# Routing jobs of a mixture-of-experts step moved into the half-swap of the attention matmuls

## The chip, the cores and the metric

The kernel runs on one core of a Trainium2 chip. The metric is the device time of one execution in microseconds (us). The engines are called as in the profile: PE (matmuls), PEld (its weight loads), DVE (vector), ACT (scalar), POOL (GpSimd) and SP (which only issues DMAs here).

## The reference, cut to what matters

Squared-ReLU attention without softmax, gated by u, is followed by a dense two-layer network and a top-1 mixture of eight experts on the same rows.

```python
# u, v: (8, 2816, 256)   z: (8, 2816, 64)
scores = (1.0 / S) * np.matmul(z, z.transpose(0, 2, 1))
attn = np.maximum(scores, 0.0) ** 2
x = (u * np.matmul(attn, v)).reshape(N, 256)         # N = 22528
y_dense = np.maximum(x @ w1_dense, 0.0) @ w2_dense    # 256 -> 512 -> 256
logits = x @ w_gate                                   # 8 experts
expert_idx = np.argmax(logits, axis=1)
gate_w = softmax(logits)[np.arange(N), expert_idx]
for e in range(8):
    mask = expert_idx == e
    y_moe[mask] = gate_w[mask, None] * (np.maximum(x[mask] @ w1[e], 0.0) @ w2[e])
out = y_dense + y_moe
```

## The kernel before, in words

The program is written out by a planner in Python, which keeps its own clock `now[0]` in microseconds and puts the instructions of PE, DVE, ACT and SP in a fixed order. On the chip each engine works through its list in that order.

**Attention.** The tokens stand in 176 blocks of 128, 22 to a batch element ("batch" below). Blocks of a batch are handled in groups of 2, 4, 4, 4, 4 and 4. A score call (`scores`, L368) makes up to 128x1024 scores with two or four matmuls on 64 rows each, into a pair of PSUM banks; there are four such pairs. `relu` (L390) then plans two steps for them, on ACT or DVE: scale and ReLU into a buffer (L398 on ACT, L400 on DVE), which frees the pair, and the square into the group's tile A (L411 on ACT, L413 on DVE). Part of A is had by transposing an earlier group's A with a DMA (L446). A score call may run up to two groups ahead of the group that is being used (`ahead`, L468).

`av` (L521) makes the output of two blocks, in a bank pair of its own. The upper and the lower 64 rows of the array work at the same time, each on its own bank, through 22 key blocks (44 matmuls, L548); in the second half (p = 1) the two swap banks. After every second key block stands a fill step (`fill`, L456). It takes up a waiting job if its time has come and a bank pair is free, or else a score call, if a pair is free and not too much is planned for DVE and ACT. `keep[0]` holds two pairs back towards the end of the first half.

Between the halves stands `swap_rows` (L499), which lies between the last matmul into a bank from one set of rows and the first from the other. It issues a touch (`touch`, L492: a matmul of 8 columns, tile d) and two score calls, the second in the touched pair. Where no score call is left to make (`ahead` is None), two touches in the same pair stand there.

DVE then multiplies the output by u (`gate_x`, L573, L577) into the ring `pays` of 22 blocks, and SP issues a DMA transpose of it to xT (L579).

**Routing.** The blocks are routed in 18 lots: 14 of 11 blocks, then 8, 6, 4 and 4. The last two are routed after the attention. `routing(q)` (L1032), called at tick `starts[q + 1] + 4`, puts a first job in the list `jobs`: the logits (L597; two matmuls of 8 columns for each block, on all 128 rows, L605). DVE works on the result (`route_a`, L611, with one exponential on ACT), and 2.5 us of the planner's time after that a second job is due: the prefix sums (`route_pre`, L631; two matmuls on 128 rows, L635 and L636). Each job holds a bank pair until DVE has read it. DVE makes the rows' places from them (`route_b`, L641; `pos`, L674), and the blocks join the list `waiting`. From there one block at a time is scattered to the experts' rows in DRAM (`scatter`, L688: a cast on DVE, L693, and an indirect DMA by POOL, L695).

`tick(g)` (L1086) runs once a block, with a timetable of further work and one scatter: for the even block between the halves, after `swap_rows` (it is handed to `av` as `between`), for the odd one after the second half. The tables of the experts' tiles (`table(0)`, L719) are made on DVE from tick `t1` on.

**Experts.** After the attention, `slot` (L954) works through tiles of 256 rows. SP fetches each transposed (L870), PE makes the hidden layers (L907) and the outputs (L915), and POOL writes the rows out (L933) and makes a small copy after some of them (L920). The blocks that are still waiting are scattered here, one in every fifth slot, each with such a copy, read from `pays`.

Of the kernel before, what the change touches and what calls it, by code (L numbers as in the profile page):

```python
# [19 lines left out]
def kernel(  # L20
# [21 lines left out]
    G = 11  # L42
# [5 lines left out]
    Q1 = nB // G - 2  # L48
# [307 lines left out]
    def room(n):  # L356

        n += keep[0]
        return len(pairs) >= n and pairs[n - 1][0] <= now[0]
# [95 lines left out]

    def fill(n, force=False):  # L456

        if jobs and jobs[0][0] <= now[0] and room(1):
            jobs.pop(0)[1]()
            return True  # L460
        m = ahead(n)
        busy = sum(1 for op in todo if op[0] in (1, 4))
        if m is not None and room(1) and busy <= (4 if n < 2 else 2):
            scores(m, left[m].pop(0))
            return True
        return False

    def ahead(n):  # L468

        for m in range(n, min(n + 3, len(groups))):  # L470
            if left[m]:
                return m if groups[m][0] in z_there else None
# [26 lines left out]
    def swap_rows(n):  # L499

        keep[0] = 0
        if ahead(n) is None:
            until(lambda: pairs[0][0] if pairs else None)
            x = take_pair()
            touch(x)
            touch(x)
            give_pair(now[0] + 0.1, x)
            return
        until(lambda: pairs[1][0] if len(pairs) > 1 else None)
        x = take_pair()  # L510
        touch(x)
        m = ahead(n)
        scores(m, left[m].pop(0))
        m = ahead(n)
        if m is None:
            touch(x)
            give_pair(now[0] + 0.1, x)
        else:
            scores(m, left[m].pop(0), x)

    def av(n, i, between):  # L521
        b, i0, w = groups[n]
        if i == i0:
            turning.extend(far_steps(n))
        keep[0] = 0
        if n == 0 and i == i0:

            fill(n)
            for g in (0, 2):
                load_u(g, gate=True)  # L530
            need(n, 0)
        until(lambda: pairs[0][0] if pairs else None)
        ox = take_pair()
        o = banks(ox, "o")
        for p in range(2):
            rest = list(range(nK))
            for x in range(nK):
                k = rest[0]
                if i == i0 and p == 0:

                    k = min(rest, key=lambda k: (key_at.get((n, k), 9e9), k))
                    need(n, k)
                rest.remove(k)
                for h in range(2):
                    r = slice(h * dq, (h + 1) * dq)
                    j = p ^ h
                    c = (i + j - i0) * P
                    nc.tensor.matmul(out=o[:, j, 0:D], lhsT=A[n][r, k, c:c + P],  # L548
                                     rhs=v_of[b][r, k, :], start=(p == 0 and x == 0),
                                     stop=(p == 1 and x == nK - 1))  # L550
                pe(0.1092)
                keep[0] = 2 - p if x >= nK - 12 else 0
                if x % 2 == 1 and x < nK - 1:
                    fill(n)
                if x % 7 == 3 and turning:
                    t = can_turn(turning[0][0] + 2, turning[0][0])
                    if t is not None and t <= now[0] and turning[0][0] + 1 in A:
                        turning.pop(0)[1]()
                if x == nK // 2 and b * nK + i + p > Q1 * G:
                    one_scatter()  # L560
            if p == 0:
                swap_rows(n)
                between()

        def done(t):
            give_pair(t + 0.1, ox)

        g = b * nK + i
        offer(now[0] + 0.2, 0, {"dve": (0.63, lambda eng: gate_x(g, o))}, done)
        keep[0] = 0  # L570
# [70 lines left out]
    def route_b(q):  # L641
# [29 lines left out]
        def three():  # L671
            nc.vector.tensor_add(inc, inc, pre[1])
            nc.vector.tensor_mul(inc, inc, oh)
            pos = vec("pos", n, bufs=3)  # L674
            nc.vector.tensor_reduce(out=pos, in_=inc.rearrange("p e t -> p t e"),
                                    axis=AX.X, op=ALU.add)
            rs[q] = pos
# [392 lines left out]
    for n, q in enumerate((nQ - 2, nQ - 1)):  # L1070
        at(nB + 2 * n, lambda q=q: late_routing(q))
        at(nB + 2 * n + 1, lambda q=q: late_places(q))
    t1 = Q1 * G + LAG + 2
    steps = table(0)
    for n, fn in enumerate(steps):
        at(t1 + n // 3, lambda n=n, fn=fn: offer(now[0], 0.5, {"dve": (0.7, lambda eng: fn())},
# [28 lines left out]
    for s in range(NT - MAYBE + 2):  # L1105
        assert s + AHEAD < NT1 or not waiting
        slot(s, NT - MAYBE)
        for fn in later.pop(nB + s, []):
            fn()
        if s % 5 == 1 and waiting:  # L1110
            g = waiting[0]
            one_scatter(dve=False)
            pause(pays[:, g % (2 * G), 0:ROW].bitcast(F32))
    assert not waiting
    assert not later
    n = nc.values_load(used[0:1, 0:1], min_val=0, max_val=NH,
                       skip_runtime_bounds_check_because="made by the table")
    with tc.If(n > NH - 2 * MAYBE):
# [33 lines left out]
```

## Time and profile before

| | us |
|---|---|
| median of 3 runs | 930.4 (929.56 to 930.82) |
| the profiled execution | 937.3 |
| its span, first to last instruction | 935.5 |
| first and last attention matmul (L548) in it | 10.8 and 581.6 |
| mean granted TensorE clock | 0.987 |

In the profile's lists a line has the start and the length in us, the engine, the line of the kernel, the operation, tiles written and read, partitions x elements, and a count where several are merged. A bracket gives the idle time of the engine before it and what ended that. Matmuls overlap: the length of a merged line runs on beyond the start of the next. In the table of stretches, each engine's busy time has its number of instructions behind it in brackets. In the list of waits stand who waited, for whom, the us in total, the number of times and the longest.

### The profile page before, as it was taken

What the parts mean: (1) busy time and instruction counts of PE and PEld (TensorE: products, weight loads), DVE (VectorE), ACT (ScalarE), POOL (GpSimd) and SP (SyncE); (2) the same over time, 40 slices, a digit from 0 to 9 for tenths busy, and PEclk for the clock granted to TensorE, in tenths of its full rate; (3) what the DMA queues carried; (4) which work ended last, traced back from release to release, by engine and by line L of the source; (5) the groups of instructions that cost most, each with busy time, mean ns of one, the idle gap of its engine ahead of it and who ended that gap; (6) DMA issues with size and microseconds to landing.
All of it is one profiled execution on the core that took longest, in us unless ns stands there. A gap on an engine that the chain in (4) does not pass through costs nothing.

```text
span 935.5 us, 30562 instructions
## 1 busy us (share of the span) xinstructions
PE 885.6 (95%) x12256; PEld 763.3 (82%) x12256; DVE 703.3 (75%) x1319; ACT 736.3 (79%) x913; POOL 489.7 (52%) x525
## 2 busy tenths in 40 slices
PE   8999999999999999999999997999899998999996
PEld 5898888888888888888887775878787887888785
DVE  6999989999999999989997972656454444446553
ACT  7999989998989989989988770667666667677664
POOL 7203343335345344344446434577777877877455
PEclk9999999999999999999999988999999999999999
DMA  7994995996997999998998745565444444434332
GB/s 139 152 181 102 164 184 112 175 200 132 178 191 133 190 179 141 193 177 142 189 188 133 140 88 91 111 123 121 100 106 106 111 111 107 117 103 95 87 91 72
DMA packets 257871, 127.64 MB, mean 136 GB/s; under 512 B 225470, under 2 KB 232894, under 8 KB 257728
## 3 DMA queue, kind: packets, MB, share of 16 engines
q1 hardware_dynamic: 230112, 70.24, 45.2%
q0 software_dynamic: 27616, 55.44, 27.7%
q8 instruction: 96, 1.57, 0.7%
q14 instruction: 47, 0.39, 0.2%
HBM read 61.54 MB, written 37.16 MB: 105 GB/s over the span
## 4 chain that ended last, share of the span: by engine, by line
PE 64%; POOL 14%; issue 12%; DVE 4%; DMA 3%; ACT 1%; POOLq 1%; SPq 0%; another core or an unknown queue 0%; DVEq 0%; ACTq 0%
PE o L548 41%; PE s L383 10%; POOL out_dram L933 9%; PE h_ps L907 6%; PE yy L915 6%; POOL zr L920 2%; DMA xT<-pays 2%; PE lg L605 1%; DVE r L400 1%; POOL A L413 1%; DVE A L413 1%; DVE ring L931 1%; DMA out_dram<-ring,ix 1%; DVE ring L895 1%; DVE pays L577 1%
## 5 line engine op out<-in xcount | busy, mean ns | idle before, releaser
L548 PE MATMUL o<-vb,A 64*128 64x256 bf16 x7744 | 501.2, 272 | 8.9 <-issue 6.0
L548 PEld LDWEIGHTS <-A 64*128 64x128 bf16 x7744 | 412.2, 95 | 62.6 <-issue 11.8
L695 POOL DMA_INDIRECT xs<-pays,pi x176 | 199.3, 1133 | 276.6 <-DVE pi L693 220.6
L398 ACT ACTIVATE r<-s 128x1024 f32<-128x1024 f32 x279 | 275.3, 1014 | 38.5 <-PE s L383 29.0
L910 ACT ACTIVATE ring<-h_ps 128x1024 bf16<-128x1024 f32 x180 | 185.6, 1032 | 95.3 <-PE h_ps L907 40.5
L411 ACT ACTIVATE A<-r 128x1024 bf16<-128x1024 f32 x252 | 256.5, 1044 | 1.7 <-DVE r L400 1.3
L413 DVE TENSOR_TENSOR A<-r 128x1024 bf16<-128x1024 f32 x172 | 208.2, 1223 | 1.1 <-ACT r L398 0.2
L931 DVE SCALAR_TENSOR_TENSOR ring<-yy,me,ring 128x256 f32<-128x256 f32 x180 | 86.1, 482 | 151.6 <-ACT ring L930 84.2
L400 DVE TENSOR_SCALAR r<-s 128x1024 f32<-128x1024 f32 (+1 forms) x153 | 185.0, 1216 | 12.3 <-PE s L383 8.3
L933 POOL DMA_INDIRECT out_dram<-ring,me x140 | 146.2, 1044 | 66.5 <-DVE ring L931 32.5
L915 PEld LDWEIGHTS <-ring 128*128 128x128 bf16 x1440 | 139.8, 98 | 38.6 <-issue 22.8
L383 PE MATMUL s<-zT 64*128 64x512 bf16 (+1 forms) x944 | 162.7, 364 | 7.1 <-remote 2.8
L915 PE MATMUL yy<-w2d,ring 128*128 128x256 bf16 x720 | 107.9, 272 | 17.3 <-DVE ring L931 15.3
L915 PE MATMUL yy<-ring 128*128 128x256 bf16 x720 | 108.0, 273 | 0.0
L907 PE MATMUL h_ps<-ring,w1d 128*128 128x256 bf16 x720 | 94.0, 273 | 3.0 <-ACT ring L910 1.3
L907 PE MATMUL h_ps<-ring 128*128 128x256 bf16 (+1 forms) x880 | 95.3, 253 | 1.4 <-issue 0.8
L895 DVE COPY ring<-wall 128x2048 bf16 x110 | 85.0, 788 | 10.4 <-issue 5.9
L930 ACT COPY ring<-yy 128x256 f32<-128x256 f32 x180 | 68.1, 378 | 30.3 <-PE yy L915 14.5
L907 PEld LDWEIGHTS <-ring 128*128 128x128 bf16 x880 | 73.4, 98 | 11.8 <-DVE ring L895 3.3
L577 DVE TENSOR_TENSOR pays<-o,ut 128x512 bf16<-128x512 f32 x88 | 61.2, 696 | 26.3 <-PE o L548 16.1
L907 PEld LDWEIGHTS <-w1d 128*128 128x128 bf16 x720 | 69.9, 98 | 12.3 <-issue 4.3
L383 PEld LDWEIGHTS <-zT 64*128 64x128 bf16 x944 | 58.5, 95 | 26.1 <-issue 15.2
(120 smaller groups left out, 359.3 us busy)
## 6 DMA issues: line engine op xcount, KB each, us to landing
ut<-in_u_dram SPq DMA_DIRECT2D x88, 256.0 KB
vb<-in_v_dram POOLq DMA_DIRECT2D x16, 384.0 KB
vb<-in_v_dram POOLq DMA_DIRECT2D x16, 320.0 KB
wall<-in_moe_w_dram POOLq DMA_DIRECT2D x16, 256.0 KB
xs<-pays,pi POOLq DMA_INDIRECT x176
zr<-in_z_dram POOLq DMA_DIRECT2D x7, 352.0 KB
out_dram<-ring,me POOLq DMA_INDIRECT x140
A<-A SPq DMA_TRANSPOSE x128
```

Of the source, the lines that this page charges most:

```text
L383: nc.tensor.matmul(out=s[:, h, y * c:(y + 1) * c], lhsT=zT[r, k + h, :], rhs=zT[r, i0:i0 + w, :], start=True, stop=True)
L398: nc.scalar.activation(r[:, :, :c], s[:, :, :c], AF.Relu, scale=1.0 / S)
L400: nc.vector.tensor_scalar(out=r[:, :, :c], in0=s[:, :, :c], scalar1=1.0 / S, scalar2=0.0, op0=ALU.mult, op1=ALU.max)
L411: nc.scalar.activation(a, r, AF.Square)
L413: (nc.gpsimd if eng == "pool" else nc.vector).tensor_mul(a, r, r)
L548: nc.tensor.matmul(out=o[:, j, 0:D], lhsT=A[n][r, k, c:c + P], rhs=v_of[b][r, k, :], start=(p == 0 and x == 0), stop=(p == 1 and x == nK - 1))
L695: ins = nc.gpsimd.indirect_dma_start(out=xs, out_offset=bass.IndirectOffsetOnAxis(ap=pi[:], axis=0), in_=pays[:, g % (2 * G), 0:ROW].bitca ...
L907: nc.tensor.matmul(out=h_ps[:, f, hs, :], lhsT=w1(c, f), rhs=xT[:, hs, c, :], start=(c == 0), stop=(c == 1))
L910: nc.scalar.activation(h, h_ps[:].rearrange("p f h t -> p f (h t)"), AF.Relu)
L915: nc.tensor.matmul(out=y[:, k, :], lhsT=h[:, f, j * P:(j + 1) * P], rhs=w2(f), start=(f == 0), stop=(f == 3))
L931: nc.vector.scalar_tensor_tensor(out=ys, in0=y[:, 1, :], scalar=me[:, j, 0:1], in1=yd, op0=ALU.mult, op1=ALU.add)
L933: ins = nc.gpsimd.indirect_dma_start(out=out, out_offset=bass.IndirectOffsetOnAxis(ap=ids[j], axis=0), in_=ys, in_offset=None, bounds_chec ...
```

## The change

Jobs are no longer taken up at fill steps. `swap_rows` looks whether a job is due; if so, it stands between two touches in the place of the two score calls, also where no score call is left. The tick of the even block now comes ahead of the swap. Three further numbers change: `pos` has four buffers, the table of the first tiles begins one tick later, and the scatters of the expert part come in every fourth slot.

```diff
@@ fill
-        if jobs and jobs[0][0] <= now[0] and room(1):
-            jobs.pop(0)[1]()
-            return True
         m = ahead(n)
@@ swap_rows
         keep[0] = 0
-        if ahead(n) is None:
+        job = jobs and jobs[0][0] <= now[0]
+        if ahead(n) is None and not job:
             until(lambda: pairs[0][0] if pairs else None)
             x = take_pair()
             touch(x)
...
         until(lambda: pairs[1][0] if len(pairs) > 1 else None)
         x = take_pair()
         touch(x)
+        if job:
+            jobs.pop(0)[1]()
+            touch(x)
+            give_pair(now[0] + 0.1, x)
+            return
         m = ahead(n)
         scores(m, left[m].pop(0))
@@ av
             if p == 0:
+                between()
                 swap_rows(n)
-                between()
@@ route_b
-            pos = vec("pos", n, bufs=3)
+            pos = vec("pos", n, bufs=4)
@@ table of the first tiles
-    t1 = Q1 * G + LAG + 2
+    t1 = Q1 * G + LAG + 3
@@ expert part
-        if s % 5 == 1 and waiting:
+        if s % 4 == 1 and waiting:
```

## The prediction

> **What bounds the kernel now.** First the page's busy times, then the stretches between 141 us and the end of the attention.
>
> ```profile
> PE 885.6 (95%) x12256; PEld 763.3 (82%) x12256; DVE 703.3 (75%) x1319; ACT 736.3 (79%) x913; POOL 489.7 (52%) x525
> ```
>
> ```profile
> core 0: us, PE busy (x) PEld busy (x) DVE busy (x) ACT busy (x) POOL busy (x), PEclk, DMA share, GB/s
> 141.00:516.00 375.00, 369.71 (x6225) 321.53 (x6221) 348.06 (x617) 343.61 (x375) 163.83 (x163) 1.00 0.99 166
> ```
>
> The columns after the stretch are its length and each engine's busy time. In the steady attention PE is busy for 369.7 of 375 us, DVE for 348.1 (93%), ACT for 343.6 (92%). So PE sets the pace, and the two engines that empty the score banks stand 7 to 8% behind it. A microsecond taken off PE's queue is a microsecond gained, as long as DVE and ACT keep up. Next the order of time on PE around one routing (start, length, line, tile, count). Lengths overlap, so I read starts.
>
> ```profile
> 200.25 0.40 PE L383 MATMUL s<-zT 64*128 64x512 bf16 x2
> 200.47 2.14 PE L548 MATMUL o<-vb,A 64*128 64x256 bf16 x36
> 202.43 0.17 PE L495 MATMUL d<-ones 64*128 64x8 bf16 x1
> 202.45 0.64 PE L383 MATMUL s<-zT 64*128 64x256 bf16 x8
> 202.92 0.40 PE L548 MATMUL o<-vb,A 64*128 64x256 bf16 x4
> ...
> 205.32 0.83 PE L548 MATMUL o<-vb,A 64*128 64x256 bf16 x12
> 206.08 0.70 PE L605 MATMUL lg<-wg,xT 128*128 128x8 bf16 x22
> 206.72 0.61 PE L548 MATMUL o<-vb,A 64*128 64x256 bf16 x8
> ...
> 208.80 0.60 PE L548 MATMUL o<-vb,A 64*128 64x256 bf16 x8
> 209.24 0.42 PE L495 MATMUL d<-ones 64*128 64x8 bf16 x2
> 209.51 1.92 PE L548 MATMUL o<-vb,A 64*128 64x256 bf16 x32
> 211.36 0.21 PE L635 MATMUL pre<-oh,ones 128*128 128x88 bf16 x1
> 211.40 0.21 PE L636 MATMUL pre<-oh,ntri 128*128 128x88 bf16 x1
> 211.54 1.05 PE L548 MATMUL o<-vb,A 64*128 64x256 bf16 x16
> ```
>
> One attention matmul takes (202.43 - 200.47) / 36 = 0.0544 us of the queue, a score call 200.47 - 200.25 = 0.22 us. From these:
> - logits: the attention is through at 205.32 + 12 x 0.0544 = 205.97 and resumes at 206.72, so a logits job costs 0.75 us;
> - prefix sums: 209.51 + 32 x 0.0544 = 211.25 to 211.54, so 0.29 us;
> - a swap with two score calls: 202.43 to 202.92, so 0.49, of which 0.44 is scores that must be made somewhere: 0.05 us of its own;
> - a swap without scores (two touches): 208.80 + 8 x 0.0544 = 209.24 to 209.51, so 0.27 us.
>
> **The change part by part.** 16 routings have two jobs each inside the attention, 32 in all. Today each job interrupts a half at a fill step and a swap is paid besides. After it, the job stands in the swap between two touches. No run has this order, so it is bounded: at least the job alone (0.75 or 0.29), at most the job plus the whole empty swap (1.02 or 0.56). The first touch is one matmul of 8 columns in the gap that stands before the logits anyway (205.97 to 206.08), and the second need not wait for the first as the empty swap's does, since the job lies between. So I take 0.77 and 0.31, near the lower end.
>
> [...]
>
> *Jobs in swaps that now hold scores.* Which swaps are empty is a count: from 66 us on there are 88 touches,
>
> ```profile
> L495 PE MATMUL d<-ones x88: 163/166/207, 68.9 to 579.3; 64*128 64x8 bf16 x88
> ```
>
> over the 80 swaps left of 88, so 8 have two. 209.24 is the swap of the very half-pair whose first half holds the logits of 206.08; routings with an odd tick (six, eight, ten, twelve repeat it a batch of 68 us later) go there. With routing 15, whose two jobs meet the last empty swaps, I count 7 jobs on empty swaps, 25 on others. On the 25 the saving is 0.75 + 0.05 - 0.77 = 0.03 us each, together -0.8. The displaced score calls cost the same 0.22 us at a fill step.
>
> *Jobs in empty swaps.* 0.75 + 0.27 - 0.77 = 0.25 us each, times 7: -1.75.
>
> *Waits for the transposed rows.* Tick now runs ahead of the swap. A job created there (even tick) is taken at once, earlier than today by the swap itself and some four fill steps (0.49 + 4 x 0.22, an estimate of 1.3 us); one created after the second half (odd tick) is taken half a pair later, 209.24 - 206.08 = 3.2 us. Two odd ones wait today, as the order on PE and, in the second fence, the windows (clock in the third figure from the right) show:
>
> ```profile
> 133.75 0.66 PE L605 MATMUL lg<-wg,xT 128*128 128x8 bf16 x20
> 135.79 0.20 PE L605 MATMUL lg<-wg,xT 128*128 128x8 bf16 x2 [1.39 <-DMA xT<-pays]
> ...
> 274.56 0.66 PE L605 MATMUL lg<-wg,xT 128*128 128x8 bf16 x20
> 275.42 0.20 PE L605 MATMUL lg<-wg,xT 128*128 128x8 bf16 x2 [0.20 <-DMA xT<-pays]
> ```
>
> ```profile
> 136.50:139.60 3.10, 3.10 (x34) 2.21 (x30) 2.40 (x6) 2.26 (x3) 0.17 (x1) 0.50 0.64 131
> ```
>
> Their 1.39 + 0.20 = 1.6 us end before the later place is reached. The first is followed by 3.1 us at a granted clock of 0.50, which is 1.55 us lost: -3.15 together. The even jobs give up 1.3 us of their margin; I charge +1.0 for one of them waiting (bounds 0 and +1.4, the longest wait here).
>
> [...]
>
> *New wait on PE.* A job swap asks for two free bank pairs where an empty one asked for one. Behind the touch stand the logits and the 44 matmuls of the second half, and DVE's gate multiply waits for those. What today's swaps wait for pairs shows as score matmuls waiting, in the same 375 us:
>
> ```profile
> PE s L383 <- PE s L383: 1.7, 7, 0.3
> ```
>
> A job in a swap needs its pair as the score call there did, so 0; bounds -1.7 (all of it gone) and +1.7 (as much again).
>
> *DVE, SP, POOL.* Routing's DVE steps move with the job, in the same number. No DMA is moved past another on SP. The scatters follow the prefix sums by up to half a pair later, and POOL is busy for 164 of 375 us: 0. The fourth buffer is memory alone. The table of the first expert tiles starts one tick (3.3 us) later. It is covered:
>
> ```profile
> 537.63 0.23 DVE L797 TENSOR_TENSOR Rt<-Rf,before 128x70 int32<-128x70 f32 x1
> ```
>
> ```profile
> 569.14 1.20 SPq L870 DMA_TRANSPOSE ring<-xs  x1
> ```
>
> 31 us lie between its end and its first reader; without that cover it would cost its 3.3 us.
>
> *Scatters in the expert part.* They come at every fourth slot, no longer every fifth.
>
> ```profile
> L920 POOL COPY zr<-pays x12: 308/317/784, 589.3 to 804.3; 128x144 f32<-128x144 f32 x12
> ```
>
> ```profile
> 611.00:630.00 19.00, 17.14 (x157) 14.97 (x155) 9.85 (x24) 11.43 (x18) 14.54 (x17) 1.00 0.60 123
> 630.00:648.00 18.00, 17.26 (x158) 15.17 (x156) 11.13 (x21) 12.92 (x20) 15.10 (x18) 1.00 0.58 124
> ...
> 822.00:841.00 19.00, 19.00 (x177) 17.00 (x175) 9.73 (x16) 12.96 (x21) 15.27 (x17) 1.00 0.41 106
> ```
>
> 12 of them are there today. Routing 15's prefix sums move from the first half to the swap, about 0.6 us later, so one scatter more (bounds 0 and 3, the room in the new pattern) falls behind the attention. Without a scatter PE does 177 matmuls in 19 us, 9.3 a microsecond; the stretches with one have 157 (2.1 us short) and 158 of 168 (1.05 us short). I take the lower, +1.1 (bounds 0 and +6.3), as other stretches also have gaps.
>
> Sum: -0.8 - 1.75 - 3.15 + 1.0 + 0 + 1.1 = -3.6 us. The profiled execution took 937.3 us (span 935.5); against it 933.7. The runs' median is 930.4, 6.9 lower, which I take off as it stands: 926.8 us.
>
> **The rivals.** *Evacuation falls behind (slower).* Ahead of each swap two pairs are kept back, so DVE and ACT finish what they have; today the swap then hands them two score calls at once. In a job swap they get none, and the next comes at the first fill step, 0.77 + 0.22 = 1.0 us later. Four jobs in a batch of 68 us make 4 us; ACT's slack there is 8%, 5.5 us. What speaks for it:
>
> ```profile
> ACT r L398 <- PE s L383: 21.5, 29, 2.3
> ```
>
> ACT already waits for scores 21.5 us in the 375. Against it: the empty swaps show that scores run up to three groups ahead once in every batch, which swallows holes. It decides when the lead is used up, seen as no empty swap left in a batch and PE waiting for A. If a third of each hole comes through: 32 x 0.33 = +10.6, 937 us. [...]
>
> *The waits only move (no change).* A bank or a transpose is late at the swap instead: the third term is lost and only -2.55 + 1.1 remains, -1.45 or 929.0 us, within the bound below.
>
> *The end of the attention resettles.* Between 511 and 571 us PE is held by things that no row names well:
>
> ```profile
> 535.00:540.00 5.00, 1.25 (x13) 0.39 (x8) 2.79 (x9) 0.08 (x1) 2.96 (x4) 0.89 0.91 187
> 563.00:572.00 9.00, 4.80 (x72) 3.07 (x66) 0.82 (x4) 0.00 (x0) 5.66 (x6) 0.87 0.47 92
> ```
>
> PE is idle for 3.75 and 4.2 us there. A shifted order can miss one (-4, 922.8 us in all) or double one (+4, 930.8).
>
> *It doesn't do what it says.* If a job's time has not come at the swap, it waits 6 us for the next, and scatters pile up behind: +3 scatters at 2.1 us, 933 us. The prefix sums are due 2.5 us after routing's DVE part, and one pair later leaves room, so this is unlikely.
>
> **How the numbers follow.** A measurement of this kernel can tell about 0.2%, 1.9 us, from no change. Forecast 0.42 (own range 924.1 to 928.4: down to no margin charged and no bank wait left, -1.0 and -1.7; up to where the bound of 1.9 us begins); resettled for the better 0.10; only moved, or resettled for the worse, 0.15; evacuation 0.27; not as said 0.06. Faster 0.42 + 0.10 = 0.52, same 0.15, slower 0.33. The range runs from 920 (the better resettling, 922.8, less the same 2.7) to 937 (a third of each hole).
>
> **What would show it.** Right: all logits and prefix sums stand directly between two touches; from the last attention matmul to the next it is 0.77 and 0.31 us; fewer swaps with two adjacent touches; no wait of logits at 134 us and full clock after it; 13 scatters behind the attention. Wrong: swaps with logits at 1.0 us; ACT's wait for scores well over 21.5 us in the same stretch, with attention matmuls waiting for A; or an attention that ends less than 3 us earlier than today.

## The result, and the profile after

| | us |
|---|---|
| changed kernel, median of 22 runs | 937.25 (928.4 to 949.4) |
| kernel before on the same chip, median of 22 runs | 929.92 (922.6 to 941.8) |
| ratio, changed to before | 1.0055, 95% interval 1.0031 to 1.0079 |
| the changed kernel's profiled execution, its span | 944.8, 943.1 |

The change costs about 5 us; 3.6 us of gain were forecast. The ratios leave disturbed executions out, the profiled one of 944.8 us among them, so here and below they are not the quotient of the medians. Both kernels spread over some 20 us from run to run. I therefore read the profiled execution beside a second one of the same kernel (the first experiment, 938.8 us, span 937.1), and where the two differ I go by the second.

First what was to get cheaper. The order of time on PE in that second execution, around one logits job and one prefix job in their swaps (start, length, line, tile, count):

```profile
238.20 2.36 PE L551 MATMUL o<-vb,A 64*128 64x256 bf16 x40
240.38 0.17 PE L492 MATMUL d<-ones 64*128 64x8 bf16 x1
240.49 0.71 PE L608 MATMUL lg<-wg,xT 128*128 128x8 bf16 x22
241.13 0.18 PE L492 MATMUL d<-ones 64*128 64x8 bf16 x1
241.14 0.41 PE L551 MATMUL o<-vb,A 64*128 64x256 bf16 x4
```

```profile
215.31 0.39 PE L551 MATMUL o<-vb,A 64*128 64x256 bf16 x4
215.52 0.17 PE L492 MATMUL d<-ones 64*128 64x8 bf16 x1
215.63 0.21 PE L638 MATMUL pre<-oh,ones 128*128 128x88 bf16 x1
215.66 0.21 PE L639 MATMUL pre<-oh,ntri 128*128 128x88 bf16 x1
215.81 0.18 PE L492 MATMUL d<-ones 64*128 64x8 bf16 x1
215.82 0.41 PE L551 MATMUL o<-vb,A 64*128 64x256 bf16 x4
```

With 0.0544 us for an attention matmul the first half ends at 238.20 + 40 x 0.0544 = 240.38 and the second begins at 241.14: 0.76 us. The prefix job takes 215.31 + 4 x 0.0544 = 215.53 to 215.82: 0.29 us. The touches and the small copies of the expert part, counted:

```profile
L492 PE MATMUL d<-ones x113: 162/166/184, 71.7 to 581.7; 64*128 64x8 bf16 x113
```

```profile
L923 POOL COPY zr<-pays x13: 309/316/322, 593.1 to 781.8; 128x144 f32<-128x144 f32 x13
```

113 touches are 2 for each of 32 job swaps and 49 for the other 48, so one swap with two touches is left of eight. All of this is as forecast. Now the stretch from 141 to 516 us, first execution and then second, with the columns of the prediction's table (length, then busy time and count of PE, PEld, DVE, ACT and POOL, clock, DMA share):

```profile
141.00:516.00 375.00, 356.57 (x6056) 316.26 (x6057) 340.24 (x604) 339.71 (x368) 171.43 (x155) 0.98 0.99 165
141.00:516.00 375.00, 364.53 (x6159) 322.83 (x6159) 344.95 (x615) 343.70 (x372) 177.09 (x161) 0.99 1.03 165
```

PE was busy for 369.7 us before (369.4 in a second execution of that kernel) and is now for 356.6 and 364.5: 5 to 13 us more of idle time. The list of waits for that stretch, of the first execution:

```profile
ACT A L411 <- DMA A<-A: 15.4, 2, 14.5
DVE A L413 <- DMA A<-A: 14.0, 2, 12.5
PE lg L608 <- DMA xT<-pays: 12.7, 2, 8.7
ACT r L398 <- PE s L383: 10.9, 27, 1.3
PE s L383 <- PE s L383: 6.5, 9, 1.0
```

and of the second:

```profile
DVE A L413 <- DMA A<-A: 7.8, 4, 3.9
ACT A L411 <- DMA A<-A: 6.1, 4, 3.6
PE s L383 <- PE s L383: 5.9, 8, 1.0
PE lg L608 <- DMA xT<-pays: 3.3, 2, 2.9
```

"ACT A L411 <- DMA A<-A" reads: the squares on ACT waited for a transpose from one A into another. Neither execution of the kernel before that I have has this wait in the stretch, and its logits waited for xT 0.2 and 0.4 us there. The new waits are transposes that come late, on both kinds of data.

The queue of SP shows what moved. Before, and then after (second execution), around the last group of a batch that is transposed (start, length of the issue, line, count):

```profile
187.96 1.53 SPq L116 DMA_TRANSPOSE zT<-zn  x1
189.58 0.88 SPq L146 DMA_DIRECT2D ut<-in_u_dram  x1
190.51 2.22 SPq L579 DMA_TRANSPOSE xT<-pays  x1
192.90 5.17 SPq L446 DMA_TRANSPOSE A<-A  x4
```

```profile
187.82 4.69 SPq L116 DMA_TRANSPOSE zT<-zn  x2
192.60 0.53 SPq L146 DMA_DIRECT2D ut<-in_u_dram  x1
193.31 1.19 SPq L446 DMA_TRANSPOSE A<-A  x1
194.56 1.26 SPq L582 DMA_TRANSPOSE xT<-pays  x1
195.86 4.68 SPq L446 DMA_TRANSPOSE A<-A  x3
```

A transpose of A stands in the queue for 1.26 us in the middle of its 128, in either kernel. The four of an A group stood together; now one goes first, an xT transpose stands behind it, and the other three leave after that. This is no accident of one execution but the order in which the program issues them. Read off the two programs for one steady batch (A with the number issued in a row, x for xT, u for ut, z for zT):

```
before  A1 x A3 u x A4 u x u x A4 z u x z u x A4 u x u x u x u x u x u
after   A4 u A1 x A3 u x u A1 x A3 u x zz u A1 x A3 u x u x u x u x u x u x
```

Before, the first of the four groups is split; after, the other three are. By the planner's code a transpose is due when the squares that it reads are planned to be done. Scores that leave a swap are made later, so the squares are later, and a new place in the list is found: behind the first transpose a gate multiply, with its xT, slips in. The split by itself does not make a wait: in batch 1 (counted from 0) the kernel before issues the same order as the changed kernel's steady batches, and no square waits there.

What a late landing does is seen best where it was worst in the second execution. SP, ACT, DVE and PE in turn; the bracket is the idle time of the engine and what ended it:

```profile
400.83 4.52 SPq L446 DMA_TRANSPOSE A<-A  x3
...
415.23 1.06 ACT L411 ACTIVATE A<-r 128x1024 bf16<-128x1024 f32 x1 [3.58 <-DMA A<-A]
...
415.27 1.23 DVE L413 TENSOR_TENSOR A<-r 128x1024 bf16<-128x1024 f32 x1 [3.87 <-DMA A<-A]
416.41 0.68 DVE L580 TENSOR_TENSOR pays<-o,ut 128x512 bf16<-128x512 f32 x1
...
417.15 0.16 PE L492 MATMUL d<-ones 64*128 64x8 bf16 x1 [1.62 <-DVE pi L696]
417.25 0.65 PE L608 MATMUL lg<-wg,xT 128*128 128x8 bf16 x20
420.76 0.21 PE L608 MATMUL lg<-wg,xT 128*128 128x8 bf16 x2 [2.86 <-DMA xT<-pays]
...
421.53 2.78 PE L551 MATMUL o<-vb,A 64*128 64x256 bf16 x24
```

ACT and DVE both stand at a square of the next batch's first scores, whose buffer the transposes still read (there are three A buffers, and by the code this one was the transposed group's). Behind DVE's square stands the gate multiply of 416.41, and PE waits first for DVE at the touch (the trace names the cast behind the gate multiply) and then for xT at the logits: 4.5 us of PE in one swap. Half clock comes on top of it: from 418.8 to 425.8 us the granted clock is 0.50, so that the 24 matmuls of the last row start 0.10 us apart and not 0.054, and 3.4 us more are lost. The batch takes 76.3 us where its neighbours take 68.3, and the two parts make up the 8 us. Between 141 and 510 us neither execution of the kernel before falls to half clock.

These three transposes had left as early as in the kernel before (9.1 us ahead of the batch's ninth pair, see the table at the end of the experiments), and the squares that needed them started 10 us after the end of their issue. So the one batch that is long is not one that the new order made late. That the load of the DMAs decides where a transpose lands late is a guess: their busy share is 1.03 here and 0.99 before. The waits of 0.9 to 1.9 us in three of this execution's other batches cost PE less than a microsecond: those batches take 68.3 to 69.0 us.

That the gate multiply stood behind the square is read off DVE's rows: it starts at 416.41, 1.14 us after the square in front of it (415.27, 1.23 us long), and the trace names nothing else that it waits for.

### The profile page after: what moved, and what is told of

Read it like the earlier page. It is cut to its first block, busy times and chain, and to the rows that moved or that the text cites. A ratio compares the mean times of both kernels' runs of the same rounds, so it can differ in the third digit from the quotient of the medians.

```text
span 943.1 us, 30629 instructions
## 1 busy us (share of the span) xinstructions
PE 878.7 (93%) x12281; PEld 769.5 (82%) x12281; DVE 705.4 (75%) x1319; ACT 740.6 (79%) x913; POOL 506.6 (54%) x526
## 4 chain that ended last, share of the span: by engine, by line
PE 75%; issue 7%; POOL 7%; DMA 4%; ACT 2%; DVE 1%; SPq 1%; another core or an unknown queue 1%; POOLq 0%; DVEq 0%; ACTq 0%
PE o L551 42%; PE s L383 11%; PE h_ps L910 10%; PE yy L918 9%; POOL out_dram L936 6%; PE lg L608 1%; DMA xT<-pays 1%; DMA vb<-in_v_dram 1%; DMA out_dram<-ring,ix 1%; SPq L446 1%; POOL zr L923 1%; ACT r L398 1%; ACT ring L913 1%; DVE ring L934 1%; DMA out_dram<-ring,me 1%
## 5 line engine op out<-in xcount | busy, mean ns | idle before, releaser
L698 POOL DMA_INDIRECT xs<-pays,pi x176 | 215.7, 1225 | 274.8 <-DVE pi L696 206.5
L398 ACT ACTIVATE r<-s 128x1024 f32<-128x1024 f32 (+1 forms) x302 | 294.5, 1014 | 27.9 <-PE s L383 21.9
L411 ACT ACTIVATE A<-r 128x1024 bf16<-128x1024 f32 (+1 forms) x229 | 233.9, 1044 | 18.1 <-DMA A<-A 15.4
L413 DVE TENSOR_TENSOR A<-r 128x1024 bf16<-128x1024 f32 (+1 forms) x195 | 233.9, 1218 | 17.1 <-DMA A<-A 14.0
L383 PE MATMUL s<-zT 64*128 64x512 bf16 (+1 forms) x944 | 164.6, 363 | 12.3 <-PE s L383 7.8
L918 PEld LDWEIGHTS <-ring 128*128 128x128 bf16 x1440 | 140.0, 98 | 37.3 <-issue 21.5
L400 DVE TENSOR_SCALAR r<-s 128x1024 f32<-128x1024 f32 (+1 forms) x130 | 157.8, 1218 | 13.9 <-PE s L383 12.4
L933 ACT COPY ring<-yy 128x256 f32<-128x256 f32 x180 | 67.9, 378 | 31.9 <-PE yy L918 18.4
L898 DVE COPY ring<-wall 128x2048 bf16 x110 | 83.8, 777 | 11.3 <-issue 4.9
```

Source lines behind the costliest of these rows:

```text
L383: nc.tensor.matmul(out=s[:, h, y * c:(y + 1) * c], lhsT=zT[r, k + h, :], rhs=zT[r, i0:i0 + w, :], start=True, stop=True)
L398: nc.scalar.activation(r[:, :, :c], s[:, :, :c], AF.Relu, scale=1.0 / S)
L400: nc.vector.tensor_scalar(out=r[:, :, :c], in0=s[:, :, :c], scalar1=1.0 / S, scalar2=0.0, op0=ALU.mult, op1=ALU.max)
L411: nc.scalar.activation(a, r, AF.Square)
L413: (nc.gpsimd if eng == "pool" else nc.vector).tensor_mul(a, r, r)
L698: ins = nc.gpsimd.indirect_dma_start(out=xs, out_offset=bass.IndirectOffsetOnAxis(ap=pi[:], axis=0), in_=pays[:, g % (2 * G), 0:ROW].bitca ...
```

## The experiments

They came in five sessions. The kernels of a session share a chip and the runs of the kernel before on it, whose medians were 927.8 (the first four below), 929.4 (the second profile of the kernel before, GpSimd's gates and two score calls), 888.2 (turn sooner, lag, numbers), 934.2 (the four on order and kind of job) and 889.2 us (the last two). Only the ratios compare across sessions.

**The changed kernel once more.**

> The changed kernel once more, beside the others on the same chip. Its first trace has two things that the trace of before has not: in some eight swaps between 170 and 500 us the matmuls stand still for 1.0 to 1.3 us (before: 0.2 to 0.5), and once, at 137 us, the logits wait 13 us for transposed rows. If the swap stalls come from the order of the program, they stand at the same places again and cost 6 to 8 us in all; if the wait of 13 us is an accident of one execution, it is gone or much shorter, and the time stays 0.3 to 0.8% above before.

Measured 1.009 (1.0057 to 1.0123). The loss holds; this is the second execution shown above.

**The tick alone.** The kernel before, with only `between()` ahead of `swap_rows(n)`; jobs stay at fill steps.

```diff
             if p == 0:
+                between()
                 swap_rows(n)
-                between()
```

> The kernel before with one part of the change: the tick ahead of the swap; jobs still at fill steps. Theory A, the stalls belong to the tick ahead of the swap (its small DVE writes and the scatter's cast now stand at the swap): swaps with stalls over 0.9 us here too, several of them, and +3 to +8 us over before. Theory B, the stalls belong to the jobs in the swaps: none over 0.7 us and the time of before within 2 us.

Measured 1.0009 (0.9975 to 1.0043): no cost that can be seen. In its list for SP one group of a steady batch is split, the first or the second by turns (in batch 2 the last too). Its profiled execution has one wait of squares for A<-A (2.5 us) and 5.7 us of score matmuls waiting for pairs.

**The tick behind the swap.** The changed kernel with the order of the kernel before there (and the table one tick later).

```diff
             if p == 0:
-                between()
                 swap_rows(n)
+                between()
```

> The changed kernel with the tick put back behind the swap (and the first table one tick later still, at t1 + 4, since routing 13 comes later). Theory A: no stalls over 0.7 us, 4 to 8 us faster than the changed kernel, so at before or up to 3 us under it. Theory B: the stalls stay, within 2 us of the changed kernel. If lateness of the routing matters, scatters behind the attention rise to 14 or 15 and cost 1 us each.

Measured 1.0248 (1.0197 to 1.0299). Now every job is a pair later, and the gate multiply waits for the scatter that still reads its ring (8.4 us, 9 times, between 141 and 516 us), with PE waiting for the gate multiply behind it (8.9 us). So lateness of routing has a price, and a plain mark in the waits; the changed kernel shows 1.4 us of it in one execution and none in the other.

**One score call given back.** The job swap ends with a score call in the touched pair, in place of the second touch.

```diff
             jobs.pop(0)[1]()
-            touch(x)
-            give_pair(now[0] + 0.1, x)
+            if ahead(n) is None:
+                touch(x)
+                give_pair(now[0] + 0.1, x)
+            else:
+                m = ahead(n)
+                scores(m, left[m].pop(0), x)
             return
```

> The changed kernel with one score call behind the job in the swap, in the place of the second touch. If ACT and DVE run dry because the job swaps give them no scores, their wait for scores falls from about 25 us to about 15 us between 66 and 592 us and the kernel gets 3 us or more faster; if the lead of the scores swallows the holes, the time stays within 2 us of the changed kernel.

Measured 1.0023 (0.9981 to 1.0065). Most of the loss is gone: 5.9 us (plus or minus 3.8) against the changed kernel beside it on the same chip. The touch that the call replaces can't be that: in the rows above the second touch starts 0.01 us before the next attention matmul. PE's busy time comes back with it, and the clock stays full:

```profile
141.00:516.00 375.00, 368.31 (x6272) 323.33 (x6269) 352.60 (x629) 346.62 (x380) 181.10 (x166) 1.00 1.01 168
```

The squares' wait for A<-A is gone from the stretch, although the steady batches' list for SP is still the one of the changed kernel. The last of the four transposes leaves 8.3 to 8.7 us ahead of the batch's ninth pair in it, against 7.3 to 7.4 us in three of the changed kernel's batches.

**The kernel before, a second profile.**

> The kernel before, one look, for a second trace of it. In its first trace the end of the attention (511 to 571 us) holds three stalls of 2 to 5 us. If they belong to its order they stand there again; if they are accidents of that execution, this trace lacks one or more of them and lies near 928 us. No square on ACT or DVE waits for the transposes of A in either case, where the changed kernel has one such wait in each batch.

923.4 us, span 921.7. The first profiled execution of before (937.3) had been one of its longer ones. The stalls at the end of the attention stand there again (the pairs begun at 528.7 and 558.3 us take 11.3 and 12.1 us, a pair else some 6), so they belong to the order. The logits' wait of 1.39 us at 135.8 us, and the half clock after it, do not.

**DVE's gates moved to GpSimd.** The changed kernel, with the one-element writes that hold back the loads of z and v (L105, L128) made by GpSimd.

```diff
-            nc.vector.memset(v_of[b][:, k0, 0:1], 0.0)
+            nc.gpsimd.memset(v_of[b][:, k0, 0:1], 0.0)
```

> The changed kernel with the small writes that hold back the loads of z and v made by POOL in place of DVE. Theory A, these DVE writes at the swap are what makes the matmuls stand still for 1.1 us once or twice a batch: those stalls go, -5 to -8 us. Theory B, they only mark the place: the stalls of about 1.1 us stay at the same swaps and the time is within 2 us of the changed kernel.

> The kernel with a job and one score call in the swap (0.65% under the changed one), with the same small writes on POOL. If both causes are real and add up: 3 to 6 us under the kernel with the score call alone, about 0.3% faster than before. If the small writes are not a cause, the same as with the score call alone, 0.2% over before.

Measured 1.0276 (1.022 to 1.0332) alone, and 1.0322 (1.0254 to 1.0389) on top of the score call given back. The swaps' stalls of 0.9 to 1.2 us, which this was to explain, stayed, so their cause is not these writes. The loads now come at another time, and the squares' wait for A<-A grows in the first of the two to 21 us on each of ACT and DVE, with 4.2 us in one place. It is the same wait as in the changed kernel, in a larger dose, at the same order of SP's queue.

**Two score calls behind the job.** As above, with a second call where the plan has a bank pair free.

> The changed kernel with up to two score calls behind the job, the second only where a bank pair is free by the plan (some ten of thirty swaps). If the missing scores are the cause, the dose counts: no wait of squares for the transposes of A, and between the time with one score call (932 us) and 3 us under it. If one call is already enough, the same as with one within 2 us.

Measured 1.0035 (0.9994 to 1.0075), no better than one. The profiled execution (954.9 us, the longest of the 13) has three waits of squares for A<-A (5.2 us at most) and three of logits for xT (5.7 us).

**Transposes offered more often.** In `av`, `x % 3 == 2` in place of `x % 7 == 3`, on the changed kernel and on the one with a score call given back.

> The changed kernel, with the transposes that build the next A buffer offered to SyncE at every third step of a half instead of every seventh, so that the four of a group leave closer together and some 1 to 2 us earlier. Late transposes: the squares' waits for A<-A of 1 to 4 us once a batch go, and with them the waits of logits that follow them; ratio to the kernel before 0.998 to 1.003, 4 to 6 us below the changed kernel. Late xT alone (the gate multiply and its transpose have too little time before the swap): the squares' waits shrink but logits at swaps still wait as much; ratio stays 1.005 or more. Neither (swap stalls of 1.1 us, or SyncE's queue as such): squares wait as before the edit or longer, because earlier transposes only stand in front of xT's; ratio 1.005 to 1.015.

> One score call given back to each job swap (as in the run that came out at 1.002), and the transposes of A offered at every third step. Late transposes: what is left of them there is little, so this gains 0 to 3 us on that run: ratio 0.997 to 1.002. If SyncE's order matters and not its lateness: 1.002 to 1.008.

Measured 1.0074 (1.003 to 1.0118) and 1.0009 (0.9967 to 1.005). The first is a miss for lateness by planning: the groups are still split in the list (the second as A2 x A2), and the squares still wait. The two kernels have the same order in SP's steady queue and differ by the score call alone, which again gains: 4.7 us (plus or minus 3.9). The second has more of the squares' wait than the first (4.7 us on DVE there), and is not told from the kernel before:

```profile
DVE A L413 <- DMA A<-A: 6.0, 3, 2.7
```

**The lots one tick later.** `LAG = 6` in place of 5 in the changed kernel.

> The changed kernel, with the routing's jobs created one tick later (LAG 6 in place of 5), so that every xT has 3.3 us more to land before its logits. Late xT: no logits in a swap waits for xT any more, 1.5 to 9 us of waits gone; ratio 0.997 to 1.002. Late transposes of A: the squares wait as before for A<-A once a batch, PE pauses there instead, and the ratio stays at 1.004 to 1.010. Too late a routing: scatters come one tick later and the gate multiply of the block 22 back starts to wait for them, as with the tick behind the swap; ratio 1.01 to 1.025.

Measured 1.0124 (1.0059 to 1.019). The logits no longer wait for xT between 141 and 516 us, so the theory that late xT is the cause had its wish, and the kernel got slower: in its profiled execution (905.8 us, the longest of six) the squares wait 6 to 8 us for A<-A, and the gate multiply 15.4 us for its scatter, as with the late tick.

**The three numbers alone.** The kernel before with four position buffers, the later table and every fourth slot.

> The kernel before with only the three numbers of the change (four buffers of positions, the table one tick later, scatters at every fourth slot of the expert part in place of every fifth). My term for the expert part was +1.1 for a 13th scatter, which this kernel should not have (12 scatters, closer together): ratio 0.998 to 1.002. If the closer spacing costs by itself what a scatter did in the stretches shown (1 to 2 us for the crowding of each), the expert part is 2 to 6 us longer: 1.002 to 1.006. If it is the cause of the whole loss, 1.005 or more.

Measured 1.0006 (0.9964 to 1.0049). They cost nothing that can be seen. With the tick alone, and if parts add up, this leaves the loss to the jobs that stand in the place of score calls; no run has the tick and the numbers together without them. The profiled execution has two waits of squares for A<-A (1.9 us at most), at the order of SP's queue that the kernel before has.

**The order of SP's queue, undone and made.** First the changed kernel, with the four transposes of a group issued at one step; then the kernel before, with three of the four held until the next xT is issued.

```diff
-                        turning.pop(0)[1]()
+                        a = turning[0][0]
+                        while turning and turning[0][0] == a:
+                            turning.pop(0)[1]()
```

```diff
+                    a = turning[0][0]
+                    due = groups[a][1] == 0 or a not in split or len(xT_made) > split[a]
-                    if t is not None and t <= now[0] and turning[0][0] + 1 in A:
+                    if t is not None and t <= now[0] and turning[0][0] + 1 in A and due:
+                        split.setdefault(a, len(xT_made))
                         turning.pop(0)[1]()
```

> The changed kernel, with all four transposes of an A group issued at the step at which the first one is (in the queue of SyncE no xT transpose stands between them any more, as in the kernel before). If the split order is the cause: no square waits for A<-A, ratio 0.997 to 1.003. If late xT is the cause: the xT that now stand behind four transposes are up to 3.8 us later, logits in swaps wait more, ratio 1.008 to 1.02. If neither: 1.005 to 1.009 as the changed kernel.

> The kernel before, with three of the four transposes of an A group held until the next xT transpose has been issued, for the groups after the first of a batch (the order that the changed kernel has, with a load of ut between as well). Jobs stay at fill steps. If the split order is the cause: squares wait for A<-A by 1 to 4 us once a batch and the ratio is 1.003 to 1.010. If it is not: 0.998 to 1.002, and the loss needs the swaps without scores themselves.

Measured 1.0058 (1.0022 to 1.0093) and 1.0064 (1.0028 to 1.0099). The second shows that SP's order alone can cost this much: PE, ACT and POOL work through the same lists as in the kernel before, and it loses as much as the changed kernel does. But its dose is larger. A load of ut and one of z's transposes stand between as well, and the last transposes leave 5.2 to 6.6 us ahead of the ninth pair, against 7.3 to 9.1 us in the changed kernel. Its five steady batches, from the start of a batch's tenth pair to that of the next, take 68.8, 72.6, 69.2, 74.6 and 68.5 us; the long ones are those with the two longest waits, 3.7 and 5.1 us, and each has a stretch at half clock (5.1 us lost in all). Its queue and its waits between 141 and 516 us:

```profile
401.79 1.26 SPq L446 DMA_TRANSPOSE A<-A  x1
403.14 0.54 SPq L146 DMA_DIRECT2D ut<-in_u_dram  x1
403.73 1.27 SPq L585 DMA_TRANSPOSE xT<-pays  x1
405.05 4.37 SPq L446 DMA_TRANSPOSE A<-A  x3
```

```profile
DVE A L413 <- DMA A<-A: 12.3, 5, 5.1
ACT A L411 <- DMA A<-A: 9.2, 5, 4.4
```

In the first, the four leave together, and there is no wait for A<-A or xT left in the stretch; these are the longest waits of ACT and PE there:

```profile
189.25 5.72 SPq L446 DMA_TRANSPOSE A<-A  x4
```

```profile
ACT r L398 <- PE s L383: 10.8, 24, 1.1
PE s L383 <- PE s L383: 7.0, 8, 1.4
```

Its steady batches take 68.6, 68.1, 67.9, 69.6 and 68.3 us, and its attention ends at 577.2 us. In the changed kernel's second execution they take 68.3, 69.0, 68.3, 76.3 and 68.3 us, to 584.1; in the first of before 68.7, 68.8, 68.4, 68.3 and 68.2 us, to 581.6. So in the changed kernel the waits go with the order. But the time did not come back with them: the ratio is still 1.0058, and nothing but SP's order differs from the changed kernel (it is not the order of before either: an xT now stands behind four transposes). In this execution the expert part takes 360.0 us, the longest of all that I have (346.0 to 356.7 in the others of these chips). The granted clock behind the attention is 0.981 in it, and 0.994 to 0.996 in both executions of before and the second of the changed kernel, which is some 5 us of it (an estimate from these shares). One execution can't say whether that belongs to the kernel.

**One kind of job in the swaps.** The logits alone, then the prefix sums alone; the other kind at fill steps.

> The changed kernel with the prefix sums at fill steps again, so that 16 swaps instead of 32 lose scores. If swaps without scores cost in proportion: 1.002 to 1.005. If the logits' late place (xT, the longer job) makes the loss: 1.005 to 1.009. If the order of SyncE's queue does: its queue has three of four groups split from the fifth batch on, two before; 1.003 to 1.008.

> The changed kernel with the logits at fill steps again and only the prefix sums in swaps. In proportion: 1.002 to 1.005. If the logits make the loss: 0.998 to 1.002. If the order of SyncE's queue does (three of four groups split from the fourth batch on): 1.003 to 1.008.

Measured 1.0012 (0.9983 to 1.0042) and 1.0046 (1.0004 to 1.0087). The intervals overlap, so that the prefix sums are the worse kind is likely and not shown. In both lists for SP the last three groups are split from the fourth batch on (not the fifth, as I had counted for the logits). The squares wait in four of the five batches with the prefix sums (up to 2.6 us), and in one with the logits (0.6 us).

**What is left.** The transposes together, and beside it either one score call given back, or the jobs of the last two lots inside the attention (14 and 15) at fill steps.

```diff
+        if jobs and jobs[0][2] >= 14 and jobs[0][0] <= now[0] and room(1):
+            jobs.pop(0)[1]()
+            return True
         m = ahead(n)
...
-        job = jobs and jobs[0][0] <= now[0]
+        job = jobs and jobs[0][2] < 14 and jobs[0][0] <= now[0]
```

> The changed kernel with one score call given back to each job swap and the four transposes of an A group issued together. If swaps without scores make the rest of the loss: no squares' waits, 0.995 to 1.001. If something else does: 1.002 to 1.006.

> The changed kernel with the transposes together and the jobs of routings 14 and 15 at fill steps as in the kernel before; the other 28 jobs in swaps without scores. If the rest of the loss is at the end: the first expert matmul waits 0.8 us for the gate multiply, 12 scatters run behind the attention, 0.997 to 1.002. If swaps without scores make it: 1.004 to 1.008, as with all jobs in swaps.

Measured 0.9964 (0.9932 to 0.9997) and 0.9973 (0.9934 to 1.0012). The first beats both kernels: 885.25 against 889.17 us. Its queue and its stretch:

```profile
187.66 5.30 SPq L446 DMA_TRANSPOSE A<-A  x4
```

```profile
141.00:516.00 375.00, 373.92 (x6382) 328.10 (x6379) 358.76 (x641) 353.28 (x387) 181.84 (x166) 1.00 1.00 170
```

PE is busy for 373.9 of 375 us, the five batches take 67.2 us each, and no job in a swap waits. (The quiet batches of the three numbers alone, on the other quick chip, take 67.3 us.) The interval of the first is barely clear of 1, and on this chip neither the changed kernel nor the one with the transposes together was run. The second is not told from no change. Its profiled execution has 9.0 us of logits waiting for xT in the stretch, in swaps without scores, and in one batch the squares wait 1.9 us although the four stand together.

One table puts the lateness and the waits side by side: for batches 2 to 6 (counted from 0), how long before the start of the batch's ninth pair the last transpose of its fourth group was issued, and the longest wait of a square for A<-A about that pair (both us, waits over 0.4).

| kernel | batch 2 | 3 | 4 | 5 | 6 |
|---|---|---|---|---|---|
| before | 9.0, none | 8.7, none | 9.1, none | 9.5, none | 8.4, none |
| changed, second execution | 7.3, 0.9 | 7.4, 1.9 | 7.4, 1.2 | 9.1, 3.9 | 8.8, none |
| changed, four together | 10.4, none | 9.8, none | 8.7, none | 11.1, none | 9.2, none |
| before, split | 5.2, 1.2 | 6.0, 3.7 | 6.6, 1.6 | 5.5, 5.1 | 6.0, 0.8 |
| score call and together | 10.5, none | 9.8, none | 10.1, none | 9.7, none | 7.7, none |

Over all 20 profiled executions, with the line drawn at 8.2 us once I had seen them: of 54 cases issued earlier 4 have a wait between 6 us before and 20 us after the ninth pair, of 46 issued later 31. In the table's execution the kernel before works 0.2 to 1.3 us on the right side of that line (one batch of its second execution stands at 7.8 us, without a wait), and the change took three of five batches to the wrong one. The longest wait of the changed kernel's row, the one that cost 8 us, is in none of those three. So the table says when squares are likely to wait, and not what the change lost.

## Why the prediction was wrong

**Jobs in swaps (0.77 and 0.31 us; -0.8 and -1.75).** Right: 0.76 and 0.30 us as the middle of 16 each in the second execution, and seven of eight empty swaps are gone. A job with the swap around it costs what the job alone had cost, so the 0.27 us of an empty swap are saved.

**Waits for the transposed rows (-3.15, and +1.0 for the margin of the even lots).** Wrong in size and side. The -3.15 was an accident of one execution: the second of before has neither the wait at 135.8 us nor the half clock, and its logits wait 0.4 us in all. The same execution's 6.9 us above the median were taken off besides. Without this term the sum is -0.45, no change that can be told. The two waits of before went, but logits waited 12.7 us in the first execution and 3.3 in the second. The margins moved as argued in direction: from the last gate multiply to the logits the odd lots have 13.7 us in the middle where they had 11.2 (3.2 more were reckoned), the even ones 14.8 for 15.1 (1.3 less were reckoned). What I left out is the other end of the margin. SP issues the odd lots' last transpose 5.5 us after its gate multiply where it took 3.8, and that eats most of the gain.

**"The displaced score calls cost the same 0.22 us at a fill step", and "No DMA is moved past another on SP."** These are the steps that failed. The first priced the lost score calls of 25 swaps at nothing beyond the place they take in PE's queue, and they cost more than that: one of them given back to the job swap gains 5.9 us, and 4.7 us on another chip, at one and the same steady order of SP. The second is right for the jobs, which issue none, and wrong for the score calls that they displace: these set when squares, gate multiplies and A transposes come up, and so their order. Such an order can cost 0.6% by itself, as the kernel before shows with a larger dose; in the changed kernel, putting the four transposes together gained nothing that can be told (1.0058). The row that should have warned me is the 5.17 us issue of four transposes in SP's queue, which I had not read.

**Bank waits at swaps (0, bounds -1.7 and +1.7).** Mis-sized: 5.9 to 7.0 us where the first execution of before had 1.7 and its second 2.9. They don't carry the sign: the tick alone has 5.7 us of them at no loss, one score call given back leaves 3.3, and in the two sessions on the quicker chips the list has no such wait in any kernel. What makes them is open.

**Scatters (+1.1).** 13 copies came as counted. Their price stays open: the closer spacing alone measured 1.0006 +- 0.004, which holds 1.1 us and zero alike.

**The rival that ended slower** had the sign, and not the mechanism. Its mark was ACT waiting for scores well over 21.5 us; ACT waited 10.9 and 11.7, and 18.7 in the quicker kernel with one score call given back. Its cause, swaps without scores, is what the runs bear out. Its condition was half met, as only one empty swap is left: the lead is used up, but the waits that then appear are for transposes and not for scores. Its size (+10.6) was too large.

**What is shown and what stays open.** Shown: the tick and the three numbers each cost nothing that can be told; giving a score call back to the job swaps gains some 5 us, twice, beside the kernel without it on the same chip; the jobs in swaps change SP's order; a later order by itself costs 0.6% in the kernel before; putting the four transposes together takes the squares' waits away (one of 15 batches in three executions still has one). In the second execution of the changed kernel and in the split one the long batches are those with a stalled swap and half clock after it. Open: by which path the missing score calls cost their time. The squares' wait for A<-A is one candidate, but it does not go with the loss: it is there at 1.0009 and 1.0006, and gone at 1.0058. Open too is why the last two runs do better. They were made on another chip, and differ from the one with the transposes together by a score call or by the last lots' jobs; the second of them keeps 28 swaps without scores at no loss that can be told, which speaks against the score calls as the whole of it. The one with the transposes together has an expert part of 360.0 us, which points to the end, but one and the same kernel varies there by 8 us (353.9 and 346.0 us in the two executions of before).

## What to carry to other kernels

Price what a moved instruction displaces, and not only what it costs itself: here the jobs were sized right to 0.01 us, and the score calls that they pushed out were put at nothing beyond their own 0.22 us. When an instruction that feeds other engines is moved, write down the order of every queue before and after, the DMA queue too; a count of what the moved piece itself issues is not enough. Do not forecast the return of a wait that one execution shows without a second one. And before such a change is given up, try it with less displaced: on another chip it came out 0.4% ahead of the kernel before with a score call left in the swap and the four transposes together.

## What the hardware showed that I had not expected

A DMA transpose of 128 KB (128x512 bf16) stands in SP's queue for 1.26 us in the middle (0.7 to 2.6 us in the first execution of before), and the four in a row of the rows above for 5.2 to 5.7 us. No row here gives the time of the transfer itself. In these kernels SP issues every DMA transpose, so no run shows what a second queue would do.

A stall of PE of 1.6 and 2.9 us, with 20 small matmuls between, was followed by 7 us at a granted clock of 0.50 in the changed kernel's second execution; neither execution of before has such a stretch between 141 and 510 us.

The chips differ by some 4.5 to 5% in the time of the kernel before, and not in the matmuls. In three of the sessions PE waits in the expert part for DVE's last step on the outputs; in the other two no such wait is left. The list of waits behind the attention, of the changed kernel:

```profile
PE yy L918 <- DVE ring L934: 16.1, 18, 1.4
```

The other chips' expert parts take 324.9 to 327.9 us where these take 346.0 to 360.0, with the same instructions: a down matmul takes 273 ns on both, DVE's last step 483 and 482 ns, and ACT's copy ahead of that step 367 and 378 ns. No row here says what the difference is.
